# Cosine without an absolute value, a one-pass weight check, state products in 64x32 tiles and half-row transposes in a fused attention and MoE kernel

## The chip, the cores and the metric

The kernel runs on one core of a Trainium2 chip. The core has TensorE (PE, matrix products into PSUM), VectorE (DVE), ScalarE (ACT), GpSimd (POOL), and SyncE (SP), whose queue issues most of the DMAs. PSUM has eight banks of 128 partitions by 512 floats. The metric is the device time of one execution in microseconds, as the median of several runs.

## The reference

An attention with a decaying state, per batch b and head h, then a two-layer MoE with the activation h cos(h):

```python
# r, k, v: (4, 8, 768, 48); w, u: (8, 48)
for t in range(768):
    cur = einsum('bhd,bhe->bhde', u * k[t], v[t])
    y[t] = einsum('bhd,bhde->bhe', r[t], state + cur)
    state = w[:, :, None] * state + einsum('bhd,bhe->bhde', k[t], v[t])
x = y as (4 * 768, 8 * 48) = (3072, 384)
h = x @ w_in            # (384, 2048), float64 input
out = (h * cos(h)) @ w_out   # (2048, 384), float64 input
```

## The kernel before

The attention works on chunks of 128 time steps of one batch, 24 in all, six for each batch. A chunk loads k, r and v (128 steps on the partitions, 8 heads by 48 columns). It needs k and r transposed (kT, rT: 112 partitions, that is a pair of heads at rows 0 to 47 and 64 to 111, by 4 pairs by 128 steps). The first 12 chunks ("early") transpose on TensorE (`tr`, L651), eight products a chunk against the identity, into two banks; DVE (L676, rT) and ACT (L711, kT) bring them out. The last 12 ("late") load k and r a second time in staged form, and DVE transposes them (L659). POOL forms r * k (L686), times u (L715), and decays k (L694). TensorE then makes the products of the chunk with itself (`mm_a`, L740, into two banks), DVE masks them into A (L746) over a diagonal that ACT has written (L730), and x of the chunk, transposed, is summed in one bank from two groups of products: `mm_x`, r on the state (L760, 12 products of 112 rows by 32 columns with the operand zt, in which ACT's two copies at L788 have spread the state so that a pair of heads is one operand), and `mm_x2`, A on v (L773, 16 products of 128 by 32). `mm_z` (L795) makes the next state, which DVE scales (`state`, L839 to L842). x is split into a rounded high part (xh, ACT, L823) and a rest (xl, DVE, L828).

The MoE runs in eight blocks of three chunks (384 columns). A step is one of 16 slices of 128 hidden units of one block, 128 steps in all: `mm_h` (L231) is nine products of 128x384 (high and rest parts of x and w_in), `mm_o` (L237) nine of them for w_out. Between them ACT and DVE make h cos(h): `whole` (qi, ACT, L242) rounds h/2pi to a whole number, `rest` (DVE, L245) forms the fraction, `size` (ACT, L248) its absolute value, `cosine` (ACT, L251) the sine of a quarter turn minus that, then the gate (DVE, L944), its rounded part gh (ACT, L947) and the rest gl (DVE, L950). The first four blocks run in turns over groups of slices, so that the weights can be made meanwhile: `conv` loads a slice of w_in or w_out as float64 words (`load_raw`, L422 and L427, 384 KB, two `raw` buffers) and makes high and rest parts on ACT, DVE and POOL. In the second half of the run `check_range` looks at all weights once more (32 slices): an absolute value on ACT (L432) and four passes on DVE (L438, L447, L456, L465) tell whether any is outside of a range; only then a general path at the end runs.

The order on each engine is fixed when the program is built: every operation is listed with a due time, a cost and the buffers that it uses, a planner simulates the engines with these figures, and the instructions are emitted in that order. Where it expects TensorE to wait before the first `mm_h`, it puts dummy products (`warm_up`, L1009), one for each 0.2 us of the expected gap:

```python
n = int(min(o.gap, 6.0) / 0.2)
```

Of the kernel before, what the change touches and what calls it, by code (L numbers as in the profile page):

```python
# [9 lines left out]
F32 = mybir.dt.float32  # L10
# [153 lines left out]
def kernel(  # L164
# [22 lines left out]
    NK = DM // P  # L187
    NF = DFF // P
# [18 lines left out]
    quarter = const.tile([P, 1], F32, name="quarter")  # L207
    nc.vector.memset(quarter, 0.5 * math.pi)
# [32 lines left out]
    def whole(qi, ph):  # L241
        nc.scalar.activation(qi, ph, AF.Copy, scale=INV_2PI)  # L242
# [4 lines left out]
    def size(q):  # L247
        nc.scalar.activation(q, q, AF.Abs)  # L248

    def cosine(q):  # L250
        nc.scalar.activation(q, q, AF.Sin, scale=-TWO_PI, bias=quarter)  # L251


    with ExitStack() as actx:
# [3 lines left out]
        bank = [Tile(banks.tile([P, 512], F32, name=f"bank{i}")) for i in range(8)]  # L258
# [8 lines left out]
        R_r = ring("r", 2, [P, H, DP], F32)  # L267
# [10 lines left out]
        R_f = ring("f", 8, [P, DM], F32)  # L278
# [3 lines left out]
        R_raw = ring("raw", 2, [P, DM, 2], I32)  # L282

        zc = [att.tile([KP, NP, D], F32, name=f"zc{b}") for b in range(B)]
        R_zt = ring("zt", 2, [KP, NP, 2 * D], F32)
# [12 lines left out]
        fine_all = att.tile([P, 2 * NF + 3], F32, name="fine")  # L300
        fine = fine_all[:, 0 : 2 * NF]
        fine_p = fine_all[:, 2 * NF : 2 * NF + 1]
        fine_m, fine_w = (fine_all[0:1, 2 * NF + i : 2 * NF + i + 1] for i in (1, 2))

# [13 lines left out]
        def start_pool2():  # L318
            for t in R_zt:
                nc.gpsimd.memset(t.ap, 0.0)  # L320
# [29 lines left out]
        b_w = Buf(B_EARLY)  # L350
        o_wT = op(PE, -95, 0.1, lambda: nc.tensor.transpose(b_w()[:, 0:NP], wr.rearrange("p j d -> p (j d)"), ident[0:NP, 0:NP]), [o_w, o_wr, o_pool], [b_w], lat=0.3)
# [67 lines left out]
        def load_raw(i, raw):  # L419
            f, part = divmod(i, 2)  # L420
            if part == 0:
# [7 lines left out]
        def check_range(i, due, behind):  # L429
            raw, ca, cb = Buf(R_raw), Buf(R_f), Buf(R_f)  # L430
            o0 = op(SP, due - 3.0, 1.6, lambda: load_raw(i, raw), [behind], [raw], lat=3.4)
            o1 = op(ACT, due, 0.47, lambda: nc.scalar.activation(ca(), f32(raw()[:, :, 1]), AF.Abs), [o0], [raw, ca])  # L432

            o2 = op(
                DVE,
                due,
                0.5,
                lambda: nc.vector.scalar_tensor_tensor(ca(), ca(), 0.0, ca(), op0=ALU.is_equal, op1=ALU.add),  # L438
                [o1],
                [ca],  # L440
                port=True,
            )
            o3 = op(
                DVE,
                due,
                0.27,
                lambda: nc.vector.tensor_scalar(cb(), ca(), F64_TINY, F64_HUGE, op0=ALU.max, op1=ALU.min),  # L447
                [o2],
                [ca, cb],
                port=True,  # L450
            )
            o4 = op(
                DVE,
                due,
                0.5,
                lambda: nc.vector.tensor_tensor(cb(), cb(), ca(), op=ALU.is_equal),  # L456
                [o3],
                [ca, cb],
                port=True,
            )  # L460
# [3 lines left out]
                0.5,  # L464
                lambda: nc.vector.tensor_reduce(fine[:, i : i + 1], cb(), op=ALU.min, axis=AX.X),  # L465
                [o4],
                [cb],
# [4 lines left out]
        def fine_min():  # L472
            nc.vector.tensor_reduce(fine_p, fine, op=ALU.min, axis=AX.X)
# [4 lines left out]
        def flag_all():  # L478
            nc.vector.tensor_reduce(fine_m, b_fine()[0:1, 0:P], op=ALU.min, axis=AX.X)
            nc.vector.tensor_tensor(flag, fine_m, fine_w, op=ALU.min)  # L480

# [76 lines left out]

        last_A = [None]
        last_z = [None] * B

# [12 lines left out]
        def chunk(i, due, xbuf):  # L577
# [221 lines left out]
            def mm_xz():  # L799
                if c:  # L800
                    mm_x()
# [360 lines left out]
```

## Time and profile before

| | before |
|---|---|
| median of 3 runs | 528.02 us (526.63 to 528.57) |
| the profiled execution | 527.78 us |
| its span | 526.1 us |
| granted TensorE clock | 0.997 |
| busy: PE, DVE, ACT, POOL | 511.6, 427.2, 394.9, 177.4 us |
| MoE products, six groups of 384 | 129.0 to 131.3 us busy each |
| DMA moved | 61.60 MB |

Busy times of PE overlap, since the next product starts while the last one still drains: the distance of two starts says what a product costs, not its recorded length. Windows give the busy time of every engine in a stretch; a group row gives the busy sum and the mean of one instruction, and behind the last bar the idle time just before it with what ended it.

### The profile page before, as it was taken

Reading aid. Unit: us, or ns where it says so; the run is one execution under the profiler, and the core shown is the slowest. Engines: PE = TensorE matmul, PEld = TensorE weight load, DVE = VectorE, ACT = ScalarE, POOL = GpSimd, SP = SyncE. Lnnn points to the kernel's source line nnn. Section 1 sums busy time; section 2 is a strip of 40 time slices with the busy share of each in tenths; the row PEclk is TensorE's granted clock in tenths of the full one; section 3 lists DMA queues with packets and bytes.
Section 4 is the critical chain, followed back from the end, with each engine's and each line's share of the span. In section 5 each row is a group of like instructions: output and inputs, shape, how many; then the busy total and the mean of one; then the engine's idle time right before and its main releaser. Section 6 shows DMA issues by size and latency. Waiting matters only on the chain.

```text
span 526.1 us, 11829 instructions
## 1 busy us (share of the span) xinstructions
PE 511.6 (97%) x4428; PEld 482.2 (92%) x4428; DVE 427.2 (81%) x835; ACT 394.9 (75%) x933; POOL 177.4 (34%) x184
## 2 busy tenths in 40 slices
PE   8999999999999999999999999899999999999995
PEld 6787799999999999999999999898999999999994
DVE  5688788889888787566899999999889998886453
ACT  3888988988888777758687787586867877776664
POOL 6766423255354244224426224404043040400000
PEclk9999999999999999999999999999999999999998
DMA  9897235667846495414584853646356453500001
GB/s 140 142 167 154 58 115 184 206 139 132 181 106 139 127 169 93 72 39 71 136 178 111 168 135 119 136 136 166 73 147 144 136 136 90 137 25 23 1 0 52
DMA packets 114979, 61.60 MB, mean 117 GB/s; under 512 B 78433, under 2 KB 110818, under 8 KB 114914
## 3 DMA queue, kind: packets, MB, share of 16 engines
q1 hardware_dynamic: 109586, 53.50, 42.2%
q0 software_dynamic: 5184, 7.08, 9.4%
q8 instruction: 36, 0.59, 0.5%
q14 instruction: 29, 0.24, 0.2%
q10 hardware_dynamic: 144, 0.20, 0.1%
HBM read 48.96 MB, written 11.80 MB: 115 GB/s over the span
## 4 chain that ended last, share of the span: by engine, by line
PE 70%; DVE 15%; ACT 8%; issue 3%; DMA 2%; POOL 1%; SPq 0%; DVEq 0%; ACTq 0%; POOLq 0%
PE bank L231 28%; PE bank L237 28%; PE bank L740 4%; PE bank L773 4%; DVE gl L950 3%; PE bank L760 2%; DVE f L944 2%; ACT A L730 2%; PE bank L651 2%; PE bank L795 1%; ACT gh L947 1%; DVE f L245 1%; DMA raw<-in_moe_w_out_dram 1%; DVE f L456 1%; ACT f L251 1%
## 5 line engine op out<-in xcount | busy, mean ns | idle before, releaser
L237 PE MATMUL bank<-w_out_hi,gl 128*128 128x384 f32 x384 | 130.7, 340 | 2.0 <-DVE gl L950 1.8
L231 PE MATMUL bank<-xh,w_in_hi 128*128 128x384 f32 x384 | 130.1, 339 | 2.1 <-DVE f L944 2.0
L237 PE MATMUL bank<-w_out_hi,gh 128*128 128x384 f32 x384 | 131.3, 342 | 0.7 <-ACT f L978 0.4
L237 PE MATMUL bank<-w_out_lo,gh 128*128 128x384 f32 x384 | 129.4, 337 | 0.0
L231 PE MATMUL bank<-xh,w_in_lo 128*128 128x384 f32 x384 | 129.4, 337 | 0.0
L231 PE MATMUL bank<-xl,w_in_hi 128*128 128x384 f32 x384 | 129.0, 336 | 0.0
L944 DVE TENSOR_TENSOR f<-bank,f 128x384 f32<-128x384 f32 (+1 forms) x132 | 71.4, 541 | 37.7 <-ACT f L251 37.1
L248 ACT ACTIVATE f<-f 128x384 f32<-128x384 f32 (+1 forms) x132 | 67.6, 514 | 39.9 <-DVE f L245 39.4
L950 DVE TENSOR_TENSOR gl<-f,gh 128x384 fp32r<-128x384 f32 (+1 forms) x132 | 85.1, 648 | 11.6 <-ACT gh L947 10.2
L947 ACT CAST gh<-f 128x384 fp32r<-128x384 f32 (+1 forms) x132 | 65.8, 500 | 31.6 <-DVE f L944 28.9
L245 DVE SCALAR_TENSOR_TENSOR f<-bank,qi 128x384 f32<-128x384 f32 (+1 forms) x132 | 70.7, 538 | 15.4 <-ACT qi L242 14.6
L242 ACT ACTIVATE qi<-bank 128x384 int32<-128x384 f32 (+1 forms) x132 | 62.1, 474 | 27.0 <-PE bank L231 26.9
L251 ACT ACTIVATE f<-f,quarter 128x384 f32<-128x384 f32 (+1 forms) x132 | 79.7, 605 | 2.2
L231 PEld LDWEIGHTS bank<-xh,w_in_hi 128*128 128x128 f32 x384 | 72.1, 188 | 4.9 <-DVE f L944 2.1
L237 PEld LDWEIGHTS bank<-w_out_hi,gl 128*128 128x128 f32 x384 | 72.0, 188 | 4.3 <-DVE gl L950 3.8
L237 PEld LDWEIGHTS bank<-w_out_hi,gh 128*128 128x128 f32 x384 | 72.0, 187 | 3.9 <-ACT f L978 1.2
L231 PEld LDWEIGHTS bank<-xl,w_in_hi 128*128 128x128 f32 x384 | 72.1, 188 | 0.2 <-DVE xl L828 0.2
L231 PEld LDWEIGHTS bank<-xh,w_in_lo 128*128 128x128 f32 x384 | 72.1, 188 | 0.0
L237 PEld LDWEIGHTS bank<-w_out_lo,gh 128*128 128x128 f32 x384 | 72.0, 188 | 0.0
L730 ACT ACTIVATE A<-ident,a 128x128 f32<-128x128 f32 x192 | 59.7, 391 | 6.3 <-DVE a L721 6.1
L664 POOL TENSOR_TENSOR kT<-kT,decT_k 112x512 f32<-112x512 f32 x12 | 16.3, 1357 | 134.7 <-DVE kT L659 99.4
L542 POOL TENSOR_TENSOR f<-f,raw 128x384 int32<-128x384 int32 x32 | 38.8, 1212 | 65.4 <-DVE f L531 22.5
(88 smaller groups left out, 678.8 us busy)
## 6 DMA issues: line engine op xcount, KB each, us to landing
raw<-in_moe_w_in_dram SPq DMA_DIRECT2D x32, 384.0 KB, 3.3
raw<-in_moe_w_out_dram SPq DMA_DIRECT2D x32, 384.0 KB, 3.2
out_dram<-f POOLq DMA_DIRECT2D x36, 192.0 KB, 5.3
k<-in_k_dram SPq DMA_DIRECT2D x24, 192.0 KB, 3.6
v<-in_v_dram SPq DMA_DIRECT2D x24, 192.0 KB, 4.2
raw<-in_k_dram SPq DMA_DIRECT2D x47, 96.0 KB, 2.4
raw<-in_r_dram SPq DMA_DIRECT2D x47, 96.0 KB, 2.3
out_dram<-f SPq DMA_DIRECT2D x23, 192.0 KB, 3.1
```

Of the source, the lines that this page charges most:

```text
L231: nc.tensor.matmul(ph, a, b_, start=(i == 0), stop=(i == len(mm) - 1))
L237: nc.tensor.matmul(acc, a[:, ts], b_[:, f, :], start=(first and i == 0), stop=(last and i == 2))
L242: nc.scalar.activation(qi, ph, AF.Copy, scale=INV_2PI)
L245: nc.vector.scalar_tensor_tensor(q, ph, INV_2PI, qi, op0=ALU.mult, op1=ALU.subtract)
L248: nc.scalar.activation(q, q, AF.Abs)
L251: nc.scalar.activation(q, q, AF.Sin, scale=-TWO_PI, bias=quarter)
L542: lambda: nc.gpsimd.tensor_tensor(ai(), ai(), cn(), op=ALU.add),
L730: nc.scalar.activation(A[j]()[:, p, :], ident, AF.Copy, scale=ab()[:, h : h + 1])
L740: nc.tensor.matmul(cube(Ap[j])[:, p, :], kT()[ps, p, :], rT()[ps, p, :], start=True, stop=True)
L944: nc.vector.tensor_tensor(g()[:, cs], ph()[:, cs], q()[:, cs], op=ALU.mult)
L947: nc.scalar.copy(gh()[:, cs], g()[:, cs])
L950: nc.vector.tensor_tensor(gl()[:, cs], g()[:, cs], f32(gh())[:, cs], op=ALU.subtract)
```

## The change

- `whole` adds 0.25 before it rounds, and `cosine` takes the sine of the full turn times the fraction plus a quarter turn; `size` is gone. Biases are plain numbers, the tile `quarter` is gone.
- `check_range`: ACT's absolute value also writes each row's sum, and one DVE pass (values under the lower limit, kept by multiplication) writes its row's sum; `fine_min` compares the sums once at the end.
- The state stays in `zc`, padded to 64 columns a pair, and is an operand itself: `mm_x` has 16 products of 48 rows by 32 columns, those of even heads (rows 0 to 47) into one bank and those of odd heads (rows 64 to 111) into another; the products with A follow in the same call, ordered by `PARTS`. zt and its copies are gone.
- With that, the features of x lie in another order on the partitions (`x_columns`), in two banks. So the copies xh and xl are three pieces each, and `load_raw` fetches w_in for `conv` with its rows in that order, in eight DMAs.
- Early chunks transpose k and r in one operation, in half rows (64 steps), the two halves into two banks; k has been decayed by then except in the first two chunks. These two banks serve nothing else in the early part, so five banks instead of seven serve the other early tiles.
- `start_banks` writes those five banks once at the start. `R_f` has nine buffers instead of eight, and `raw` a third one, which lies in the memory of the two r buffers and is free when the early chunks are done. Some planned costs differ.

```diff
     def whole(qi, ph):
-        nc.scalar.activation(qi, ph, AF.Copy, scale=INV_2PI)
+        nc.scalar.activation(qi, ph, AF.Copy, scale=INV_2PI, bias=0.25)
-    def size(q):
-        nc.scalar.activation(q, q, AF.Abs)
     def cosine(q):
-        nc.scalar.activation(q, q, AF.Sin, scale=-TWO_PI, bias=quarter)
+        nc.scalar.activation(q, q, AF.Sin, scale=TWO_PI, bias=0.5 * math.pi)
...
-        B_EARLY = bank[5:8] + bank[3:5] + bank[0:2]
+        B_EARLY = bank[5:8] + bank[3:5]
+        B_TR = [Tile(both)]
...
-        R_f = ring("f", 8, [P, DM], F32)
+        R_f = ring("f", 9, [P, DM], F32)
-        R_raw = ring("raw", 2, [P, DM, 2], I32)
+        R_raw = ring("raw", 2, [P, DM, 2], I32) + [raw_r]
...
+            o1 = op(ACT, due, 0.55, lambda: nc.scalar.activation(
+                    ca(), f32(raw()[:, :, 1]), AF.Abs, accum_out=fine[:, i : i + 1]), [o0], [raw, ca])
+            return op(DVE, due, 0.55, lambda: nc.vector.scalar_tensor_tensor(
+                    cb(), ca(), F64_TINY, ca(), op0=ALU.is_lt, op1=ALU.mult,
+                    accum_out=fine[:, 2 * NF + i : 2 * NF + i + 1]), [o1], [ca, cb], port=True)
...
+            def tr():
+                for at, src in enumerate((kb, rb)):
                     for p in range(NP):
-                        nc.tensor.transpose(d[0:KP, p, :], flat(src, p), ident)
+                        for i in range(2):
+                            rows = slice(i * C // 2, (i + 1) * C // 2)
+                            a0 = at * DM_T + p * C // 2
+                            nc.tensor.transpose(
+                                trp()[0:KP, i, a0 : a0 + C // 2], flat(src, p)[rows], ident[rows, rows])
...
             def mm_x():
-                x = xv()
-                for g in range(NK * 4):
-                    p, s = divmod(g, 3)
-                    gs = slice(G * (g % 4), G * (g % 4) + G)
-                    nc.tensor.matmul(
-                        x[gs, g // 4, :], zb()[:, p, G * s : G * s + G], rT()[0:KP, p, :], start=(g < 4), stop=False,
+                if c:
+                    for n, (h, skip, i, at, g) in enumerate(PARTS):
+                        p, j = divmod(h, 2)
+                        ps = slice(j * DP, j * DP + D)
+                        e0 = p * DP + skip
+                        nc.tensor.matmul(
+                            xv(i)[G * g : G * g + G, at, :],
+                            zc[b].rearrange("q p e -> q (p e)")[ps, e0 : e0 + G],
+                            rT()[ps, p, :],
+                            start=(n < 8),
...
+            def x_parts():
+                top = slice(P // 2, P)
+                return (
+                    (slice(0, P), slice(0, 2), xv(0)),
+                    (top, slice(1, 2), xv(1)[top, 0:1]),
+                    (slice(0, P), slice(2, 3), xv(1)[:, 1:2]),
+                )
```

How instructions move shows in the order of three engines. A row has the line, the instruction, and the tiles written and read with buffer numbers (`both` is the pair of banks for transposes, `r_all` the two r buffers). TensorE before, at an early chunk:

```order
L651 MATMUL bank_85<-ident,k_89 112x128 x4
L651 MATMUL bank_78<-ident,r_86 112x128 x4
L760 MATMUL bank_81<-rT_98,zt_126 32x128 x12
L740 MATMUL bank_82<-rT_99,kT_97 128x128
L740 MATMUL bank_79<-rT_99,kT_97 128x128
```

TensorE now, at such a chunk (L711 are the transposes, L839 the state products, L850 those with A, L1081 the dummies):

```order
L1081 MATMUL bank_77<-warm 128x256
L711 MATMUL both<-ident,k_86 112x64 x8
L711 MATMUL both<-ident,r_all 112x64 x8
L839 MATMUL bank_81<-rT_95,zc_119 32x128 x4
L839 MATMUL bank_79<-rT_95,zc_119 32x128 x4
```

The transposes are twice as many of half the width, and the state's products go alternately to two banks, four strips each. Before the first `mm_h` there are 102 dummies of 256 columns (70 before) and five of 512.

SP's queue before, where the first slice of w_in is loaded among the chunks' loads:

```order
L609 DMA r_86<-in_r_dram 128x8x48
L422 DMA raw_120<-in_moe_w_in_dram 128x3x256
L593 DMA v_92<-in_v_dram 128x8x48
L593 DMA k_90<-in_k_dram 128x8x48
L609 DMA r_87<-in_r_dram 128x8x48
```

SP's queue now:

```order
L647 DMA v_88<-in_v_dram 128x8x48
L446 DMA raw_117<-in_moe_w_in_dram 64x1x256
L446 DMA raw_117<-in_moe_w_in_dram 32x1x256 x2
L446 DMA raw_117<-in_moe_w_in_dram 64x1x256 x2
L446 DMA raw_117<-in_moe_w_in_dram 32x1x256 x2
L446 DMA raw_117<-in_moe_w_in_dram 64x1x256
L647 DMA k_86<-in_k_dram 128x8x48
```

The load has become eight issues, and it stands ahead of the sixth chunk's loads; before it stood behind the k load of the eighth and the r load of the ninth.

DVE before, where weights are checked (L245, L944, L950 are the MoE's three operations of a step):

```order
L438 SCALAR_TENSOR_TENSOR f_112<-f_112 128x384
L950 TENSOR_TENSOR gl_118<-f_114,gh_116 128x384
L721 TENSOR_REDUCE a_94<-f_111 128x8
L447 TENSOR_SCALAR f_114<-f_112 128x384
L438 SCALAR_TENSOR_TENSOR f_107<-f_107 128x384
L456 TENSOR_TENSOR f_114<-f_114,f_112 128x384
L944 TENSOR_TENSOR f_108<-bank_83,f_108 128x384
L465 TENSOR_REDUCE fine<-f_114 128x1
```

DVE now (L244, L1017 and L1023 are those three, L482 the check):

```order
L1017 TENSOR_TENSOR f_111<-bank_79,f_111 128x384
L1023 TENSOR_TENSOR gl_116<-f_111,gh_114 128x384
L244 SCALAR_TENSOR_TENSOR f_108<-bank_80,qi_112 128x384
L482 SCALAR_TENSOR_TENSOR f_103,fine<-f_106 128x384
L1017 TENSOR_TENSOR f_108<-bank_80,f_108 128x384
```

A check stood in four places between a step's operations, and stands in one now.

More of the change, by code (lines that the diff above doesn't have):

```diff
@@ L431, in check_range @@
             o0 = op(SP, due - 3.0, 1.6, lambda: load_raw(i, raw), [behind], [raw], lat=3.4)
-            o1 = op(ACT, due, 0.47, lambda: nc.scalar.activation(ca(), f32(raw()[:, :, 1]), AF.Abs), [o0], [raw, ca])
-            o2 = op(
-                DVE,
-                due,
[L437 to L459, printed above, removed]
+            o1 = op(
+                ACT,
+                due,
+                0.55,
+                lambda: nc.scalar.activation(
+                    ca(), f32(raw()[:, :, 1]), AF.Abs, accum_out=fine[:, i : i + 1]
+                ),
+                [o0],
+                [raw, ca],
             )
@@ L557, in conv @@
             return o8
+        PARTS = []
+        for t in range(2):
+            for j in range(2):
+                for g in range(4):
+                    some = [(*x, j, kk - j, g) for kk in range(NK) for _, x in x_columns(kk, g) if x[0] % 2 == j]
+                    PARTS.append(some[t])
         last_A = [None]
+        tr_first = [Buf([t]) for t in bank[0:2]]
+        r_first = Buf([raw_r])
         last_z = [None] * B
@@ L732, in diagonal @@
                 return go
-            o_d = [op(ACT, due - 1.55 + 0.01 * j, 0.9, diagonal(j), [o_a, o_pool], [ab, A[j]], line="diagonal") for j in range(2)]
+            o_d = [op(ACT, due - 1.55 + 0.01 * j, 1.18, diagonal(j), [o_a, o_pool], [ab, A[j]], line="diagonal") for j in range(2)]
             def mm_a():
```

258 lines of the change are left out of this document (152 added, 106 removed), and 3 rows, old and new, of the table b_fine.

## The prediction

> **What bounds the kernel now.** I read the page's busy times first, then the engines by stretch (cut at 64.3 us, where the MoE's first product starts, and at 519.8 us, where its last one does), then TensorE's waits.
>
> ```profile
> PE 511.6 (97%) x4428; PEld 482.2 (92%) x4428; DVE 427.2 (81%) x835; ACT 394.9 (75%) x933; POOL 177.4 (34%) x184
> ```
> The stretches: length, then busy us (instructions) of PE, its weight loads, DVE, ACT, POOL; clock, DMA share, GB/s.
> ```profile
> 0.00:64.30 64.30, 60.55 (x1075) 47.86 (x1075) 48.04 (x103) 48.13 (x140) 41.56 (x56) 1.00 0.75 134
> 64.30:519.80 455.50, 450.72 (x3360) 434.32 (x3355) 378.75 (x733) 346.29 (x792) 135.81 (x128) 1.00 0.50 115
> 250.00:450.00 200.00, 196.87 (x1742) 186.74 (x1742) 184.47 (x344) 147.79 (x343) 59.88 (x54) 1.00 0.56 135
> ...
> 513.45 1.56 PE bank L231 x9
> ...
> PE bank L231 <- DVE f L944: 2.0, 3, 1.3
> PE bank L237 <- DVE gl L950: 1.8, 3, 0.9
> PE bank L237 <- ACT f L978: 0.4, 1, 0.4
> PE bank L237 <- DVE f L980: 0.2, 1, 0.2
> ```
> PE is busy 450.7 of the 455.5 us between the cuts, at clock 1.00. Nine MoE products start within 1.56 us (a piece of the chain), 0.174 each; there are 6 x 384 of them, so 2304 x 0.174 = 401 us of the span is MoE work that the change leaves as it is. What it can win lies in the first 64 us, in PE's attention work, and in PE's idle time: 4.8 us between the cuts. A stall hides its first part there, since a product is recorded as 0.34 us long (below) while the next starts 0.17 after it; the last four rows (waits: sum, times, longest) have 8 stalls on MoE products, so I add 8 x 0.17 = 1.3 and take 6.1 us as all that can be had from stalls. Most sit in 250 to 450, where DVE is busy 184.5 of 200 us.
>
> **The change part by part.** *State by r.* TensorE in order of time (start, length, records):
> ```profile
> 228.35 0.34 PE L237 MATMUL bank<-w_out_lo,gh 128*128 128x384 f32 x1
> 228.62 0.86 PE L760 MATMUL bank<-rT,zt 112*32 112x128 f32 x24
> 229.30 1.08 PE L773 MATMUL bank<-A,v 128*32 128x128 f32 x32
> ...
> 39.40 0.65 PE L651 MATMUL bank<-ident,k 128*112 128x128 f32 x4
> 39.88 0.60 PE L651 MATMUL bank<-ident,r 128*112 128x128 f32 x4
> 40.41 0.86 PE L760 MATMUL bank<-rT,zt 112*32 112x128 f32 x24
> 41.21 1.16 PE L740 MATMUL bank<-rT,kT 48*128 48x128 f32 x16
> ...
> 40.41 0.32 PE L760 MATMUL bank<-rT,zt 112*32 112x128 f32 x4
> ```
> The 24 records of L760 take 0.68 us when L773 follows with the same 32-column tiles, and 0.80 when a product of another tiling follows: 0.12 for the change of tiling. The last row is cut to 0.03 us: four records, one per column strip, had started in it, so a group goes in packs of four, 24/4 = 6 packs in 0.68, 0.11 each. After, 16 products (32 records) of 48 rows by 32 columns sit in eight places (two row halves, four strips, each half with its own bank): 32/8 = 4 packs, 0.44, and 0.02 to start, and now always a change of tiling before the products with A, 0.12: 0.58. A late chunk wins 0.10 (12 of them: 1.2 us), an early one 0.80 - 0.58 = 0.22 (7 before the MoE starts: 1.5). Packs of eight are not in this trace; if no more than four went together it would be 8 packs, 0.88 + 0.14, a loss of 0.34 a late chunk. I take eight, since L740 already runs its two row halves together: 16 records of 128 columns from 41.21 in 1.1 us, two per 0.11 pack plus entry.
>
> *Transposes.* k and r of an early chunk cost 40.41 - 39.40 = 1.01 us now, eight full ones at 0.11. After, 16 of half the rows, which stream 64 columns: half of 0.11, 0.055. In pairs 8 x 0.055 + 0.17 for entry and change of tiling = 0.61; one by one 16 x 0.055 + 0.17 = 1.05. I take the pairs, again by L740: 0.40 x 12 = 4.8 us less, between -0.04 x 12 = 0.5 more and 4.8.
>
> The Trainium skill (TensorE: Matmul & The Clock Gate, LDWEIGHTS) gives a weight load's time as its columns over 1.2 per ns. That would be 112/1.2 = 93 ns a pair here, an estimate, 0.91 a chunk, and the sum below would be 3.6 us smaller in gain; no row separates the two, since every 128-column product here already streams for 0.11.
>
> *Dummy products.* The program has 102 instead of 70 warm-up products, and five wide ones that clear the banks at the start, where PE waits for w's load and powers anyway.
> ```profile
> 17.00 0.72 PE L1009 MATMUL bank<-warm 128*128 128x256 bf16 x5
> 17.56 0.60 PE L651 MATMUL bank<-ident,k 128*112 128x128 f32 x4
> ...
> 64.38 0.44 PE L231 MATMUL bank<-xh,w_in_hi 128*128 128x384 f32 x1
> ```
> Five take 17.56 - 17.00 = 0.56, so 32 more are 32 x 0.11 = 3.5 us. They stand where the order expects PE to wait. If the waits come they cost nothing, if not all 3.5; I count them in full, because PE was busy 60.6 of 64.3 us there. The first stretch, which ends with the last row, then changes by -4.8 - 1.5 + 3.5 = -2.8, between -6.3 and the loss in the second rival.
>
> *Other engines.* Groups (busy us, mean ns):
> ```profile
> L248 ACT ACTIVATE f<-f 128x384 f32<-128x384 f32 (+1 forms) x132 | 67.6, 514 | 39.9 <-DVE f L245 39.4
> L438 DVE SCALAR_TENSOR_TENSOR f<-f 128x384 f32<-128x384 f32 x32 | 18.0, 564 | 0.6 <-ACT f L432 0.6
> L447 DVE TENSOR_SCALAR f<-f 128x384 f32<-128x384 f32 x32 | 11.2, 352 | 0.1
> L456 DVE TENSOR_TENSOR f<-f,f 128x384 f32<-128x384 f32 x32 | 20.3, 635 | 0.1
> L465 DVE TENSOR_REDUCE fine<-f 128x1 f32<-128x384 f32 x32 | 17.2, 540 | 0.1
> L788 ACT COPY zt<-zc 48x192 f32<-48x192 f32 x40 | 13.9, 348 | 1.4 <-PE bank L760 1.1
> L823 ACT CAST xh<-bank 128x384 fp32r<-128x384 f32 x24 | 11.3, 469 | 2.8 <-PE bank L773 2.6
> ...
> 517.20 0.29 ACT L248 ACTIVATE f<-f 128x128 f32<-128x128 f32 x1
> ```
> The absolute value goes: 67.6 us of ACT, and 0.51 from each step's chain from h to o; ACT has idle time, so on the path this is worth only the stalls, and at the end, where the last part's 0.29 stands in the chain, 0.3. The check of weights falls from four DVE passes to one: 18.0 + 11.2 + 20.3 + 17.2 - 32 x 0.564 = 48.7 us of DVE, all in 250 to 450, which brings its 184.5 towards 136. Sums along the row inside an instruction aren't in the trace: between nothing and one pass like L465, 0.54, so at most 17 us on each of ACT and DVE, still a relief. The copies of the state go (13.9 of ACT). The x copy becomes three pieces; a piece of 128 columns costs 0.29, so three are at most about 1.0 instead of 0.47, 12 us more on ACT and as much on DVE, covered by the above late; early ACT's 11 x 0.5 is balanced by the state copies, and DVE's is covered by its idle time (48.0 of 64.3 busy). The biases as numbers and the padded state cost nothing that a row shows. Of the 6.1 us of stalls I take 5: their releasers are DVE and ACT work, and both get lighter, but an order fixed ahead always leaves some. Bounds: 0 and 6.1.
>
> *Loads of w_in.* Eight DMAs in place of one, for 16 loads, on SP's queue.
> ```profile
> 188.29 1.81 SPq L614 DMA_DIRECT2D raw<-in_r_dram  x4
> 63.93 0.37 SPq L422 DMA_DIRECT2D raw<-in_moe_w_in_dram  x1
> SPq L422 <- POOL f L542: 41.4, 13, 10.5
> ```
> Four issues of a staged load took 1.81, so eight take 3.6 instead of 0.37. Behind them in SP's queue wait w_out's loads, output stores and, once, the sixth chunk's loads. I cost it at nothing: the queue itself waits 41.4 us for buffers at this line, and a third raw buffer lets it start earlier. Without that cover it is the third rival.
>
> **Sum.** -2.8 (first stretch) - 1.2 (late state) - 5.0 (stalls) - 0.3 (end) = -9.3 us. The profiled execution took 527.8 (span 526.1), 0.2 under the median of 528.0, so 518.5.
>
> **The rivals.** *First stretch in full:* if the dummies only fill waits, -6.3 instead of -2.8: 515.0. For it: they are placed by expected waits. Against: ACT and DVE are also busy 48 of 64 us and stand in each chunk's chain.
>
> *First stretch gains nothing:* r now stays in its buffer (two of them) until k has been decayed and both are transposed.
> ```profile
> L694 POOL TENSOR_TENSOR k<-k,dec_k 128x384 f32<-128x384 f32 x24 | 26.8, 1118 | 1.2
> L686 POOL TENSOR_TENSOR f<-r,k 128x384 f32<-128x384 f32 x12 | 12.4, 1032 | 10.5 <-DMA r<-in_r_dram 5.3 <-DMA k<-in_k_dram 3.2 <-DVE A L746 1.9
> ```
> POOL already waits 5.3 us for r. One decay, 1.1, per turn of the two buffers is five turns, 5 us at most; also five banks instead of seven serve the other early tiles. I take +2 in place of -2.8: 523.3 (with +5, 526.3). Against: r's transposes already ran late, in PE's order.
>
> *Slower: w_in arrives late.* If the eight issues push w_in behind the step that needs it, PE stalls 15 times after 64 us. The change loses once each load holds PE for (9.3 + 2.6)/15 = 0.8 us; at half of the 3.2 us extra it is 15 x 1.6 - 9.3 = +14.7, 542.7. Against: the waits for POOL above, which show slack at this queue.
>
> *No eightfold packs:* records then follow at a floor. The trace speaks against one near 25 ns, with four starts inside 0.03 us. At 0.025, 32 records are 0.80 + 0.12, 0.24 more a late chunk than now: +2.9 in place of -1.2, so 522.6. The Trainium skill (TensorE: Matmul & The Clock Gate, Part 1) states such a floor of about 25 ns between starts; its Part 3 has 4 ns within a pack, which is the one that this trace bears out for strips.
>
> **How the numbers follow.** A change under 0.5% (2.6 us) can't be told from none here. Forecast 0.48 (515 to 522 by its own bounds), first stretch in full 0.20, no gain there 0.17, no packs 0.06, late w_in 0.05, mixtures 0.04. Faster than 525.4 are the first two and nearly all of the third and fourth: 0.90; same 0.05; slower 0.05. The range is 511 (both gains at their ends: 6.3, 1.2, 6.1, 0.4 make 514, and 3 for stalls that I don't see) to 525 (no gain early, stalls stay in part).
>
> **What would show it.** The MoE's first product near 61.6 us; a late chunk's state products in 0.58 us with L773's successor after that; transposes of a chunk in 0.61; DVE busy below 150 of 200 us in 250 to 450, and PE's idle time between the cuts below 2 us; no group for the absolute value, and ACT about 70 us lighter. The forecast is wrong if the first product is at or after 64, if state products come in packs of four, or if MoE products wait for w_in.

## The result and the profile after

The changed kernel takes 589.83 us (median of 4 runs, 588.75 to 590.65) against 527.40 before on the same chip: ratio 1.118, interval 1.115 to 1.121. The forecast was 518.5, range 511 to 525. The profiled execution has a span of 587.7 us and a granted clock of 0.955. Busy times, then the chain that ended last, by engine and by line, from the page of the kernel after:

```profile
PE 527.6 (90%) x4721; PEld 490.9 (84%) x4721; DVE 395.6 (67%) x820; ACT 328.4 (56%) x841; POOL 178.2 (30%) x186
PE 63%; DMA 17%; SPq 7%; DVE 5%; POOL 3%; issue 2%; ACT 1%; DVEq 0%; POOLq 0%; ACTq 0%
PE bank L230 26%; PE both L236 18%; PE bank L236 9%; DMA raw<-in_moe_w_in_dram 8%; SPq L446 7%; DMA r_all<-in_moe_w_in_dram 4%; PE bank L818 3%; PE bank L850 3%; DMA r_all<-in_r_dram 2%; DMA raw<-in_moe_w_out_dram 2%; PE bank L839 1%; POOL f L583 1%; DMA r_all<-in_moe_w_out_dram 1%; DMA k<-in_k_dram 1%; PE bank L863 1%
```

PE is 90% busy where it was 97%, and w_in's loads with their issues (L446) are 8 + 7 + 4 = 19% of the chain. The engines by stretch, kernel after, cut at the first MoE product and at the end of the last; the columns are those of the prediction's windows:

```profile
0.00:68.40 68.40, 60.15 (x1232) 45.61 (x1232) 51.82 (x115) 43.68 (x134) 40.86 (x57) 0.98 0.75 126
68.40:578.90 510.50, 467.07 (x3495) 445.21 (x3489) 343.19 (x706) 284.23 (x706) 137.37 (x129) 0.96 0.43 103
64.00:100.00 36.00, 25.57 (x323) 21.36 (x301) 23.46 (x53) 18.21 (x49) 9.42 (x9) 0.81 0.25 75
100.00:250.00 150.00, 116.95 (x583) 111.40 (x584) 91.90 (x187) 75.62 (x172) 50.13 (x49) 0.90 0.47 116
250.00:450.00 200.00, 199.88 (x1749) 190.94 (x1748) 143.07 (x287) 117.82 (x300) 58.07 (x55) 1.00 0.53 115
```

The first product comes 4.1 us later, the part between the cuts is 510.5 - 455.5 = 55.0 longer, and what follows the last product 2.5. The loss lies ahead of 250 us, while weights are being made: the 658th MoE product starts at 249.9 us instead of 184.0, 65.9 later, and the last one is 59.1 later, so 6.8 are won back behind it. In the windows from 64 to 250 PE is idle for 43.5 us, and the clock of 0.81 and 0.90 takes up to 36 x 0.19 + 150 x 0.10 = 21.8 us more, an estimate. From 250 to 450 PE is busy 199.9 of 200, better than before.

Waits of all engines from 64 to 250 us (sum, times, longest), kernel after:

```profile
ACT raw L552 <- DMA raw<-in_moe_w_in_dram: 29.8, 7, 7.1
PE bank L236 <- DVE gl L1023: 20.1, 8, 6.5
DVE f L560 <- DMA raw<-in_moe_w_in_dram: 15.1, 4, 7.2
DVE f L560 <- DMA r_all<-in_moe_w_in_dram: 13.8, 3, 5.6
```

The engines that make the weights wait for w_in; the MoE's steps stand behind them on ACT and DVE, so gl is late, and PE is charged to gl. SyncE's queue in order of time (start, length), kernel after:

```profile
82.64 4.95 SPq L446 DMA_DIRECT2D r_all<-in_moe_w_in_dram  x8
87.69 0.43 SPq L461 DMA_DIRECT2D raw<-in_moe_w_out_dram  x1
89.50 7.38 SPq L446 DMA_DIRECT2D raw<-in_moe_w_in_dram  x8
97.04 1.08 SPq L461 DMA_DIRECT2D r_all<-in_moe_w_out_dram  x1
98.22 2.27 SPq L1063 DMA_DIRECT2D out_dram<-f  x3
100.64 6.68 SPq L446 DMA_DIRECT2D raw<-in_moe_w_in_dram  x8
```

A load of w_in holds the queue for 5.0 to 7.4 us in these rows, and for up to 9.1 in others, where it held it for 0.37; in the 24.7 us shown the queue rests for 1.9.

### The profile page after: what moved, and what is told of

It is laid out like the page before. It is cut to its first block, busy times and chain, and to the rows that moved or that the text cites. A ratio compares the mean times of both kernels' runs of the same rounds, so it can differ in the third digit from the quotient of the medians.

```text
span 587.7 us, 12700 instructions
## 1 busy us (share of the span) xinstructions
PE 527.6 (90%) x4721; PEld 490.9 (84%) x4721; DVE 395.6 (67%) x820; ACT 328.4 (56%) x841; POOL 178.2 (30%) x186
## 4 chain that ended last, share of the span: by engine, by line
PE 63%; DMA 17%; SPq 7%; DVE 5%; POOL 3%; issue 2%; ACT 1%; DVEq 0%; POOLq 0%; ACTq 0%
PE bank L230 26%; PE both L236 18%; PE bank L236 9%; DMA raw<-in_moe_w_in_dram 8%; SPq L446 7%; DMA r_all<-in_moe_w_in_dram 4%; PE bank L818 3%; PE bank L850 3%; DMA r_all<-in_r_dram 2%; DMA raw<-in_moe_w_out_dram 2%; PE bank L839 1%; POOL f L583 1%; DMA r_all<-in_moe_w_out_dram 1%; DMA k<-in_k_dram 1%; PE bank L863 1%
## 5 line engine op out<-in xcount | busy, mean ns | idle before, releaser
L230 PE MATMUL bank<-xh,w_in_hi 128*128 128x384 f32 x384 | 132.5, 345 | 6.8 <-ACT w_in_hi L588 4.1
L1023 DVE TENSOR_TENSOR gl<-f,gh 128x384 fp32r<-128x384 f32 (+1 forms) x132 | 78.6, 599 | 30.2 <-ACT gh L1020 29.9
L244 DVE SCALAR_TENSOR_TENSOR f<-bank,qi 128x384 f32<-128x384 f32 (+1 forms) x132 | 70.9, 540 | 29.5 <-ACT qi L241 29.1
L236 PE MATMUL both<-w_out_hi,gh 128*128 128x384 f32 x256 | 89.1, 348 | 1.4 <-DVE f L1052 1.1
L1017 DVE TENSOR_TENSOR f<-bank,f 128x384 f32<-128x384 f32 (+1 forms) x132 | 70.9, 540 | 27.3 <-ACT f L247 25.6
L236 PE MATMUL both<-w_out_hi,gl 128*128 128x384 f32 x256 | 88.7, 346 | 0.0
L236 PE MATMUL both<-w_out_lo,gh 128*128 128x384 f32 x256 | 88.3, 345 | 0.0
L236 PE MATMUL bank<-w_out_hi,gl 128*128 128x384 f32 x128 | 45.5, 356 | 20.1 <-DVE gl L1023 20.1
L236 PE MATMUL bank<-w_out_hi,gh 128*128 128x384 f32 x128 | 45.8, 358 | 11.9 <-ACT f L1050 6.8
L236 PEld LDWEIGHTS both<-w_out_hi,gh 128*128 128x128 f32 x256 | 49.5, 193 | 3.1 <-DVE f L1052 1.9
L236 PEld LDWEIGHTS both<-w_out_hi,gl 128*128 128x128 f32 x256 | 49.7, 194 | 0.0
L236 PEld LDWEIGHTS both<-w_out_lo,gh 128*128 128x128 f32 x256 | 49.7, 194 | 0.0
```

The costliest lines, as they stand in the source:

```text
L230: nc.tensor.matmul(ph, a, b_, start=(i == 0), stop=(i == len(mm) - 1))
L236: nc.tensor.matmul(acc, a[:, ts], b_[:, f, :], start=(first and i == 0), stop=(last and i == 2))
L244: nc.vector.scalar_tensor_tensor(q, ph, INV_2PI, qi, op0=ALU.mult, op1=ALU.subtract)
L1017: nc.vector.tensor_tensor(g()[:, cs], ph()[:, cs], q()[:, cs], op=ALU.mult)
L1023: nc.vector.tensor_tensor(gl()[:, cs], g()[:, cs], f32(gh())[:, cs], op=ALU.subtract)
```

## The experiments

**What the loads of w_in cost: four runs.** In the first, each load is one DMA as before, which leaves out the row order that x needs; all else, the order of the work too, is the changed kernel's. (The other runs whose expectations say that rows meet x in the wrong order leave it out too.)

```diff
-            o0 = op(SP, due - 3.5, 1.6 if part else 2.7, lambda: load_raw(i, raw, True), [behind], [raw], lat=3.4)
+            o0 = op(SP, due - 3.5, 1.6 if part else 2.7, lambda: load_raw(i, raw), [behind], [raw], lat=3.4)
```

> The changed kernel with w_in loaded for the conversion by one DMA of 128 x 3 x 1 KB, as in the kernel before (so the weights' rows meet x in the wrong order; the work is the same). Everything else stands in the same order. Theory E: each of the eight DMAs with rows in two runs goes through one of the sixteen DMA engines, some 47 GB/s, so a 384 KB load takes 7 to 8 us and SP's queue stands still behind it. Theory I: the eight issues themselves cost SP 0.6 to 0.9 us each. Theory O: the loss comes from another part of the change (the order, the banks, the clock). E and I: 511 to 522 us, near the forecast. O: still above 570 us.

Measured: 527.76 us against 526.85, ratio 1.002 (1.000 to 1.003). The whole loss is in these loads, and theory O is out; but what else the change brings nets to nothing, so the 511 to 522 us of E and I are missed. The second keeps the rows in the order that x needs, with each two-run DMA split into two of evenly spaced rows, 16 a load:

```diff
-                            bass.AP(tensor=w_in_w.tensor, offset=..., ap=[[(c1 - c0) * rl, 2], [rl, 16 * n], [1, 2 * P]]),
+                        for half, cc in ((0, c0), (1, c1)):   # one DMA each, 16 * n rows from row cc
```

> The changed kernel with every one of the eight DMAs of a w_in load split in two, so that each has one run of 16 or 32 evenly spaced rows (sixteen issues a load, same bytes, same rows, full result). Theory E: the engines share each DMA again, a load takes as long as its sixteen issues, 16 x 0.37 = 6 us of SP's queue at most: 515 to 535 us, far below the changed kernel. Theory I: twice the issues, so the loss doubles: 620 us or more. Theory O: 585 to 595.

Measured: 567.64, ratio 1.080 (1.077 to 1.083): twice the issues, and still 22 us faster than two-run DMAs. It lies between the forecasts of E (at most 535) and I (at least 620), so neither is enough alone. The other two put eight DMAs a load into the kernel before, nothing else: two-run ones, and plain ones of the same sizes.

```diff
-            o0 = op(SP, due - 3.5, 1.6, lambda: load_raw(i, raw), [behind], [raw], lat=3.4)
+            o0 = op(SP, due - 3.5, 1.6, lambda: load_raw(i, raw, True), [behind], [raw], lat=3.4)   # load_raw as changed
```

> The kernel before with the changed kernel's eight DMAs of two row runs in each w_in load, and nothing else of the change (its weights' rows so meet x in the wrong order). E and I: the loss of the change alone, 570 to 595 us. O: 525 to 535.

```diff
+                for kk in range(NK):
+                    for r0, n in (((0, 64), (64, 32), (96, 32)), ((0, 64), (64, 64)), ((0, 32), (32, 32), (64, 64)))[kk]:
+                        ...   # one DMA: rows kk * P + r0, n of them, evenly spaced
```

> The kernel before with each w_in load in eight DMAs of the same sizes (32 or 64 rows of 1 KB), but each with evenly spaced rows. Theory E: 526 to 533 us, since the sixteen engines share each. Theory I: as slow as with two-run DMAs, 570 to 595. It separates the number of issues from their row pattern.

Measured: 647.61, ratio 1.229 (1.226 to 1.232), and 554.53, ratio 1.054 (1.048 to 1.059). Eight DMAs in place of one cost 27.7 us, the two-run pattern 93 us more. Both figures miss their forecasts (570 to 595 for the first run, 526 to 533 or 570 to 595 for the second): each theory has a part of the loss, and the pattern is the larger one. The changed kernel loses 62 us to the DMAs that cost the kernel before 121. It has a third raw buffer, but which of its differences helps was not tried.

**What makes a two-run load slow.** The same eight DMAs with four runs of half as many rows:

```diff
-                                ap=[[(c1 - c0) * rl, 2], [rl, 16 * n], [1, 2 * P]],
+                                ap=[[24 * rl, 4], [rl, 8 * n], [1, 2 * P]],
```

> The kernel before with each load of w_in for the conversion by eight DMAs of the same sizes as in the two-run test, but with four runs of half as many rows in each (w_in's rows come in a wrong order; times alone are read). The two-run test took 647.6 us, eight DMAs of evenly spaced rows 554.5. Theory K (the outer count of the pattern sets how many DMA engines carry it; the two-run loads moved about 48 GB/s at a DMA share of 0.13, two of sixteen): with four, the share is 0.25 and the rate about double, so a load takes about 4.1 us, what its issues take anyhow, and the time comes near 554.5: 553 to 575 us. Theory G (any pattern with a gap goes through the same narrow path): 640 to 650 us. The Trainium skill (DMA: Bandwidth & Descriptors, the section on why a DMA increments its semaphore by 16) states theory K: the largest number up to 16 that divides the slowest dimension of both patterns.

Measured: 580.4, ratio 1.100 (1.097 to 1.102). Of the 93 us, 67 are gone: nearer to theory K, though its 575 is missed. A load's issues take the same time in both (SyncE's queue, first the two-run kernel, then the four-run one), but the next load starts 14.7 us later in the one and 10.7 to 11.3 in the other (8.8 to 9.9 with eight plain DMAs, from 77.1 us, and 8.0 to 8.7 in the kernel before, from 74.3 us):

```profile
91.31 4.94 SPq L441 DMA_DIRECT2D raw<-in_moe_w_in_dram  x8
105.98 4.96 SPq L441 DMA_DIRECT2D raw<-in_moe_w_in_dram  x8
```
```profile
78.12 5.10 SPq L441 DMA_DIRECT2D raw<-in_moe_w_in_dram  x8
88.81 5.12 SPq L441 DMA_DIRECT2D raw<-in_moe_w_in_dram  x8
100.09 5.12 SPq L441 DMA_DIRECT2D raw<-in_moe_w_in_dram  x8
```

Windows within such loads, last columns clock, DMA share and GB/s: two runs, four runs, and one plain DMA (the single-load kernel).

```profile
92.50:95.50 3.00, 3.00 (x19) 2.82 (x18) 2.82 (x7) 2.96 (x8) 0.00 (x0) 1.00 0.12 37
```
```profile
79.50:82.50 3.00, 3.00 (x19) 2.82 (x18) 2.83 (x8) 2.96 (x8) 0.00 (x0) 1.00 0.22 68
```
```profile
73.50:74.50 1.00, 1.00 (x5) 1.00 (x4) 0.71 (x2) 0.00 (x0) 0.63 (x1) 0.50 0.87 308
```

0.12 of sixteen engines are 1.9 (so two, not theory E's one), 0.22 are 3.5, 0.87 are 13.9. 384 KB at 37 GB/s take 10.6 us, at 308 1.3. In the kernel after, by the packets in its trace, a load of w_in is under way for 8.5 to 11.7 us, in the single-load kernel for 1.8 to 3.2; from 84.0 to 158.3 us seven loads are under way for 65 of the 74 us. The Trainium skill (DMA: Bandwidth & Descriptors, the section on why a DMA increments its semaphore by 16) says that a DMA runs on the largest number of engines up to 16 that divides the slowest dimension of both address patterns. The trace agrees: the slowest dimension of the source is 2 and then 4.

**The row order that x needs, by evenly spaced rows only.** Twelve DMAs a load (four of 32 rows for two slices of x at once, eight of 16 rows), first with half of them on ACT's queue, then all on SyncE's:

```diff
+                for kk, u, c in ((0, 0, 0), (0, 2, 7), (1, 4, 3), (1, 6, 10)):
+                    q_.dma_start(rr[16 * u : 16 * u + 32, kk : kk + 2], ...ap=[[2 * DFF, 32], [12 * 16 * 2 * DFF, 2], [1, 2 * P]])
+                for kk, u, c in ones:   # eight
+                    q_.dma_start(rr[16 * u : 16 * u + 16, kk], w_in_w[16 * c : 16 * c + 16, fs_])
```

> The changed kernel with its complete result, each load of w_in by twelve DMAs of evenly spaced rows (four of 32 rows for two slices at once, eight of 16 rows), six on SyncE's queue and six on ScalarE's. Theory Q (what the changed kernel lost is SyncE's queue, at 0.5 us an issue, and the rate of a two-run DMA): SyncE spends 3 us a load, ScalarE 3 us more a load, 48 us in all on an engine with 200 us idle: 530 to 540 us. Theory A (a ScalarE that issues DMAs holds the cosines behind them): over 550 us.

> The changed kernel with its complete result and its own order, each load of w_in by twelve DMAs of evenly spaced rows, all on SyncE's queue. With six of the twelve on ScalarE's queue it took 550.2 us, with sixteen on SyncE's 567.6. Theory A (ScalarE's issues held the cosines behind them): one queue is faster than two, 540 to 548 us. Theory Q (SyncE's queue is the limit, 12 times 0.41 is 4.9 us a load): 552 to 560 us.

Measured: 550.20, ratio 1.040 (1.036 to 1.044), and 545.07, ratio 1.031 (1.026 to 1.036). One queue is the better one, as theory A has it (the first run reaches its "over 550" by 0.2), but the first run's plan also ordered the work anew, so the cause isn't isolated. This is the change as fast as it got with its own row order: 45 us better than as made, 3% slower than before.

**The parts that need no other row order.** The kernel before with the new cosine alone, and with the new check of the weights too:

```diff
-        nc.scalar.activation(qi, ph, AF.Copy, scale=INV_2PI)
+        nc.scalar.activation(qi, ph, AF.Copy, scale=INV_2PI, bias=0.25)
-                o3 = op(ACT, dd + 0.7, 0.44 * one, f_size, [o2], [q], line="size", lat=0.1)
-                o4 = op(ACT, dd + 0.8, 0.44 * one, f_cos, [o3], [q], line="cos")
+                o4 = op(ACT, dd + 0.8, 0.52 * one, f_cos, [o2], [q], line="cos")
```

> The kernel before with one part of the change: the cosine without the absolute value. Its result is complete. Theory S (the stalls of MoE products come from ScalarE's and VectorE's chain from h to o, so a shorter chain removes them): with 0.51 us less per step the waits of MoE products, 6.1 us, fall by about half, and 0.3 goes at the end, 523.5 us. Theory N (the single-load run of the changed kernel showed no gain, because its parts only trade one wait for another): within 0.5% of before, 525 to 529 us.

The second adds the change's `check_range`, with the lower sums in a table that is free by then:

```diff
+        low = qk.rearrange("q p n -> q (p n)")[:, 0 : 2 * NF]
+                    accum_out=low[:, i : i + 1],
```

> As the run with the cosine alone, and also the weights' range by row sums, one pass of VectorE for four. Its result is complete. Theory S: VectorE falls from 184 of 200 us to about 140 between 250 and 450, the waits between the first and the last MoE product go almost whole, 521.5 us (5.0 for stalls, 0.3 at the end, 0.6 at the start unknown). Theory N: the same as with the cosine alone, or within 0.5% of before.

Measured: 525.60, ratio 0.995 (0.994 to 0.997), and 522.86 against 528.04, ratio 0.990 (0.988 to 0.992). The first gain is clear of noise, but about half of what theory S asked, and 525.60 lies in theory N's band: alone it does not decide. The second decides for S. It is faster than both kernels. Its stretches, cut at its first and after its last MoE product, and the one wait of a MoE product on PE that is left between the cuts:

```profile
0.00:64.40 64.40, 61.34 (x1075) 48.92 (x1075) 48.20 (x102) 48.17 (x141) 41.54 (x56) 1.00 0.74 134
64.40:512.40 448.00, 446.80 (x3359) 435.17 (x3353) 334.18 (x672) 284.39 (x692) 134.88 (x128) 1.00 0.49 117
512.40:520.80 8.40, 0.30 (x2) 0.00 (x0) 0.36 (x1) 0.48 (x1) 0.00 (x0) 0.69 0.23 79
```
```profile
PE bank L235 <- DVE gl L937: 1.2, 1, 1.2
```

The middle is 455.5 - 448.0 = 7.5 us shorter; 2.1 are lost again behind the last product (8.4 us for 6.3).

**Where the gain of the rest went.** The single-load kernel has less work on PE in each chunk, and yet gained nothing. Its way from the first product to the 129th took 32.6 us for 24.7 (95.8 us and 89.1 on the clock of the span); from there to the end of the MoE it was 8.8 us faster than before, and behind the last product 3.4 slower: 6.7 - 8.8 + 3.4 = +1.3, the difference of the spans (the profiled execution is the slowest of its ten, 1.4 above their median). Windows of the single-load kernel, after one of the kernel before:

```profile
68.00:72.00 4.00, 4.00 (x24) 4.00 (x25) 2.93 (x8) 3.13 (x8) 0.92 (x1) 1.00 0.22 85
```
```profile
68.00:72.00 4.00, 1.47 (x34) 0.88 (x26) 3.82 (x12) 2.55 (x7) 2.48 (x2) 0.97 0.56 174
72.00:76.00 4.00, 3.41 (x11) 3.42 (x12) 2.45 (x7) 1.84 (x5) 1.21 (x1) 0.50 0.41 125
76.00:80.00 4.00, 4.00 (x18) 4.00 (x17) 3.38 (x9) 2.81 (x8) 1.21 (x1) 0.68 0.38 106
```

PE waits for the second slice of w_in, and then runs at half the clock for some 6.6 us, by the clocks of the last two windows. Two runs tried the place of that slice in the plan, by the time booked for a load and by the due times:

```diff
-            o0 = op(SP, due - 3.5, 1.6 if part else 2.7, ...
+            o0 = op(SP, due - 3.5, 1.6, ...
```

> The changed kernel with one DMA for each load of w_in, as in the first single-load run, but with the load booked in the plan at 1.6 us of SyncE's queue as before, so the order is made anew (w_in's rows meet x's columns in the wrong order; times alone are read). The first single-load run lost 7.9 us in its first 128 MoE products, to waits for the second slice of w_in and a clock of 0.50 after them. Theory B (the booking of 2.7 us pushed the second slice's conversions back): with 1.6 they come earlier, the waits at 68 to 73 us and the low clock go, about 520 us. Theory D (they come late because VectorE carries the x copies in three pieces and the transposed k and r there): the same waits, 526 to 529 us.

```diff
-                due = 2 * i - 3.0
+                due = 2 * i - 3.0 + {1: 4.0, 2: -4.0}.get(i, 0.0)
```

> The first single-load run of the changed kernel, with the due times in the plan of w_in's second slice 4 earlier and of w_out's first slice 4 later, nothing else (w_in's rows meet x's columns in the wrong order; times alone are read). Theory L (the 7.9 us lost in the first 128 MoE products are the wait for the second slice and the low clock behind it): PE waits no longer than 1 us between 64 and 75, the clock stays at 1.00, those products take about 25 us, 520 us in all. Theory W (all of the work before 80 us is too much for VectorE, GpSimd and the loads, and the wait only stands somewhere else): the first product comes later, or the waits move, and the time stays between 525 and 529 us.

Measured: 534.44, ratio 1.011 (1.008 to 1.015), a miss for both theories, since the plan pulled the first MoE step to 44.4 us and the rest came later; and 528.61, ratio 1.002 (1.000 to 1.004). There the clock stayed at 1.00 and no wait on PE between 60 and 97 us was over 1.1, and still the 129th product came at 95.4, no better: theory W. The wait and the low clock were signs of a first stretch that is too full, not its cause. Three runs of the kernel before then priced that stretch: PE with more work (each early transpose twice), PE without its dummies, and ACT and DVE with the x copies in three pieces.

```diff
+                    for _ in range(2):
                         for p in range(NP):
                             nc.tensor.transpose(d[0:KP, p, :], flat(src, p), ident)
```

> The kernel before with each early transpose of k and r done twice over, in the same order and with the same result: 12 chunks with 8 more transposes at 0.11 us, 10.6 us more on PE in the first stretch. Theory P (the step of the prediction: PE's attention work sets the first stretch, so 0.40 us less per chunk is 4.8 us less): first product about 10 us later, 537 us. Theory W (other engines set it, and the dummy products hide it on PE): first product under 3 us later, 527 to 531 us.

```diff
-                    n = int(min(o.gap, 6.0) / 0.2)
-                    if n:
-                        warm_up(n)
```

> The kernel before without its 70 dummy products, all else in the same order and with the same result. Theory P (PE sets the first stretch): 70 times 0.11 is 7.7 us less there, 520 us. Theory W: PE idles where they stood, and the time is the same within 0.5%, unless the granted clock falls below 1.00 in the stretch, which would make it slower by some us.

```diff
+                for kk in range(NK):
+                    nc.scalar.copy(xbuf()[0][:, kk], xv()[:, kk])   # and the same for DVE's rest
```

> The kernel before with the copies of x by three pieces of 128 columns on ScalarE and on VectorE, as the changed kernel has them, in the same order and with the same result. Each chunk gets about 0.6 us more on each of the two. Theory W (VectorE and ScalarE set the first stretch): the first product and the first 128 after it come 3 to 7 us later in sum, 530 to 534 us. Theory C (covered, as the prediction has it): within 0.5% of before.

Measured: 533.26, ratio 1.013 (1.010 to 1.015); 528.52, 1.003 (1.001 to 1.005); 531.09, 1.007 (1.004 to 1.010). The first lies between the forecasts of P and W, the second is W's, the third W's by its time. Without dummies PE is busy 54.5 of 64.3 us instead of 60.6, and the first product comes 0.7 us later, not 7.7 earlier:

```profile
0.00:64.30 64.30, 54.48 (x985) 43.45 (x989) 48.77 (x102) 47.43 (x138) 41.90 (x56) 1.00 0.78 134
```

Of the 10.6 us of added transposes the first product feels 7.5. So dummies that are taken away there turn into waits, while work that is added costs most of its length: PE and the engines around it are about equally long in this stretch. The three-piece copies cost 0.9 us in it, so their time is not lost where theory W has it; in the profiled execution, the slowest of its six, some 5 us more came between 310 and 355 us, where DVE was still full in that kernel.

The single-load kernel without dummies (the same edit), and then with r transposed on its own, ahead of k's decay:

> The first single-load run of the changed kernel without its dummy products, all else in the same order (w_in's rows meet x's columns in the wrong order; times alone are read). It shows which waits the dummies cover. Theory H (the first stretch is slow because r and k are transposed together, after GpSimd has decayed k): PE's waits before 80 us stand mostly at the transposes, for k from GpSimd, 5 us and more. Theory V (the three-piece copies and the rest of VectorE's chain): they stand mostly at the products behind VectorE and ScalarE. In both the time is 526 to 530 us, as the dummies only fill waits, unless the clock falls.

```diff
-        B_TR = [Tile(both)]
+        B_TR = [[Tile(both[:, :, at * DM_T : (at + 1) * DM_T])] for at in range(2)]
+                t_r = op(PE, due - 2.5, 0.3, tr(1, rb), [l_r, o_pool], [*rbs, trp[1], rT, *tr_first], lat=0.3)
```

> The first single-load run of the changed kernel with r's half-row transposes as a step of their own, which does not wait for k's decay, into their own half of the two banks; the first MoE step is kept behind the ninth chunk, so that it stays near 63 us (w_in's rows meet x's columns in the wrong order; times alone are read). Theory H: r's buffers come free earlier, the next loads too, and the first stretch with the 128 products after it gets 3 to 6 us shorter: 522 to 525 us. Theory V: it changes less than 1.5 us, 526 to 529 us.

Measured: 536.28, ratio 1.017 (1.014 to 1.020), and 531.48, ratio 1.008 (1.005 to 1.011); both lie above all of their forecasts. The clock fell in the first one. Its waits on PE ahead of 80 us, and two windows:

```profile
PE bank L818 <- ACT kT L788: 5.5, 5, 2.0
PE bank L818 <- DVE rT L768: 3.8, 3, 1.9
```
```profile
20.00:40.00 20.00, 16.53 (x364) 13.38 (x360) 15.40 (x35) 14.92 (x48) 11.23 (x13) 0.91 0.81 150
40.00:64.30 24.30, 19.79 (x448) 16.06 (x448) 18.73 (x41) 17.16 (x53) 13.33 (x13) 0.79 0.62 118
```

The dummies covered a new wait: the chunk's own products (L818) wait 9.3 us for the copies of the transposes, behind ACT and DVE as theory V has it. The kernel before without dummies waits 3.0 us there. That r and k now come out of the banks together, and late, could be the reason. But r apart, with a plan of its own order, did not bring the time back (129th product at 97.7 us), so theory H is not borne out, though the new order leaves it untested by itself. In the single-load kernel DVE is busy 23.0 of the 24.3 us before 64.3; in the kernel before 20.0:

```profile
40.00:64.30 24.30, 23.55 (x607) 18.91 (x600) 23.00 (x49) 19.75 (x64) 13.15 (x13) 1.00 0.62 121
```
```profile
40.00:64.30 24.30, 23.69 (x501) 18.74 (x499) 19.96 (x41) 21.81 (x64) 14.64 (x14) 1.00 0.51 109
```

This points to DVE (theory V), whose x copies there take 1.15 us for 0.56, but no run showed that taking it away brings the time. What holds the first stretch of the single-load kernel stays open between these two.

## Why the prediction was wrong, point by point

**Loads of w_in: the step that failed.** "I cost it at nothing: the queue itself waits 41.4 us for buffers at this line, and a third raw buffer lets it start earlier." Two mistakes stand in it. First, the wait for a buffer isn't slack: a load cannot start before its buffer is given back, so its issues and its transfer lie behind that wait, in the same loop of buffer, load, conversion, buffer. What lengthens a piece lengthens the loop. Second, only the issues were priced (3.6 us; plain ones took 4.3 to 5.1, two-run ones 5.0 to 9.1), and the transfer was taken as it was, though its address pattern changed: 8.5 to 11.7 us where one DMA took 1.8 to 3.2. The page of the Trainium skill cited above (DMA: Bandwidth & Descriptors) has the rule for the engines, and it was not weighed.

**The slower rival** had the mechanism and a chance of 0.05. Its point of decision, 0.8 us a load, was passed far: the loss against the single-load kernel is 62 us, 3.9 for each of the 16 loads, above even the whole 3.2 that it allowed, because it knew only the issues.

**First stretch (-2.8).** The sizes were right. TensorE in order of time, kernel after:

```profile
43.76 0.67 PE L839 MATMUL bank<-rT,zc 48*32 48x128 f32 x32
44.35 1.08 PE L850 MATMUL bank<-A,v 128*32 128x128 f32 x32
45.37 0.44 PE L711 MATMUL both<-ident,k 64*112 64x64 f32 x8
45.64 0.39 PE L711 MATMUL both<-ident,r_all 64*112 64x64 f32 x8
45.96 0.28 PE L1081 MATMUL bank<-warm 128*128 128x256 bf16 x1
```

A chunk's transposes take 45.96 - 45.37 = 0.59 (0.61 forecast) and state products 0.59 (0.58). The Trainium skill's weight-load time (TensorE: Matmul & The Clock Gate, LDWEIGHTS) would have made the transposes 0.91, an estimate; the trace does not agree here. The step that failed here took PE's work for the length of the stretch, because PE was busy 60.6 of 64.3; but 6 us of that were dummies, put where PE waits, and the other engines' chain is about as long. With one load the first product came 1.2 us earlier, not 2.8, and the next 128 gave it all back and 6.7 more.

**Late state (-1.2)** fits: a late chunk's state products take 0.60 us (318.81 to 319.41 in the kernel after) where they took 0.68, so 12 x 0.08 = 1.0. The rival without eightfold packs is out: 32 records in 0.60 instead of its 0.92.

**Stalls (-5.0)** were mis-sized on the safe side: cosine and check alone give 7.5 between the cuts, more than the 6.1 that the prediction took as all that can be had. PE's idle time there fell by 3.6, from 4.8 to 1.2, and its busy time by 3.9, from 450.7 to 446.8: if that is the part that stalls hid, it was put at 1.3. 250 to 450 in the kernel after was as forecast, DVE 143 (below 150) and PE idle 0.1; over the whole run ACT is 66.5 us lighter. The check's pass costs what the row did that it was taken from (medians 551 and 550 ns; the means, 614 and 564, differ by a few long ones), and the sine is cheaper than it was; groups after, and the sine's before:

```profile
L482 DVE SCALAR_TENSOR_TENSOR f<-f 128x384 f32<-128x384 f32 x32 | 19.6, 614 | 0.4 <-ACT f L471 0.4
L247 ACT ACTIVATE f<-f 128x384 f32<-128x384 f32 (+1 forms) x132 | 67.3, 513 | 44.6 <-DVE f L244 43.0
```
```profile
L251 ACT ACTIVATE f<-f,quarter 128x384 f32<-128x384 f32 (+1 forms) x132 | 79.7, 605 | 2.2
```

The 92 ns less per sine, which the prediction costed at nothing ("biases as numbers"), are 12 us of ACT. The Trainium skill (ScalarE: Activation LUTs, What ACT_TABLE_LOAD costs) gives about 93 ns for each operand that is read from a tile; the trace agrees.

**End (-0.3)**: the place that it was priced at lies ahead of the last product. There the products pause for 0.4 us in the kernel before (517.84 to 518.78 us for three starts that take 0.53 elsewhere) and not in the kernel after, so the term may well have come about. What follows the last product, which the sum left as it was, moves by more. It took 6.3 us before, 8.8 in the kernel after, and 8.4 to 9.7 in the single-load kernel and the two with parts alone; but also 7.9 in the kernel before with eight plain DMAs, which has none of those parts, and 6.2 in the changed kernel with twelve on one queue, which has all of them. So this growth is not shown to come from the change.

## What to carry to other kernels

A wait at the head of a DMA queue says that a buffer came late, not that the DMA may take longer: price issue and transfer inside the loop of the buffer. When an access pattern changes, look at how many DMA engines the trace shows busy during it, and keep a large, evenly divided dimension outermost; here an irregular order of rows cost 62 us as it was made, and 3% of the time in the fastest form found, for state products whose gain on PE is 1.2 + 1.5 = 2.7 us by the prediction. An engine that is 94% busy need not be the bound if part of that is filler: take the filler out before pricing what is saved there.

## What the runs showed of the hardware that was not expected

- DMAs of 32 and 64 KB in two runs use 0.12 of the sixteen engines, in four runs 0.22, and one of 384 KB by even rows 0.87.
- One stretch of 4 us with PE busy 1.5 was followed by a clock of 0.50 for the next 4 us and 0.68 for the 4 after. The kernel before kept 1.00 without dummies, the single-load one fell to 0.91 and 0.79.
- Behind the last product, the single-load kernel's stores have all landed 4.5 us later, and the span ends another 5.1 us after that; only packets of the instruction queues move then. In the kernel before, the same two parts take 4.5 and 1.8 us. Why the second differs between builds was not tried.
